# One-hots of two heads turned together, 128 columns wide, with the work of the first batch placed anew

## The chip, the cores and the metric

The kernel runs on one core of a Trainium2 chip. A core has five engines that run side by side and wait for each other through semaphores: TensorE (PE, matmuls; weight loads are listed as PEld), VectorE (DVE), ScalarE (ACT), GpSimd (POOL) and SyncE (SP), which here only issues DMAs. Each engine works through its own instructions in the order in which the program gave them. Matmuls write to PSUM, which only VectorE and ScalarE of the other engines read here. The metric is the device time of one execution in microseconds (us); the kernel before took 343.95 us (median of three runs, 343.53 to 344.48).

## What is computed

Four batches of eight attention heads with 768 queries and keys of 64 elements, followed by a gated feed-forward network (FFN). Every query and every key is assigned to the nearest of 16 centroids of its head, and a query only attends to keys with the same centroid:

```python
q_assign = np.argmax(np.einsum('bhsd,hcd->bhsc', q_n, c_n), axis=-1)
k_assign = np.argmax(np.einsum('bhsd,hcd->bhsc', k_n, c_n), axis=-1)
mask = q_assign[:, :, :, None] == k_assign[:, :, None, :]
scores = np.where(mask, scale * np.matmul(q, k.transpose(0, 1, 3, 2)), -1000000000.0)
attn = softmax(scores);  x = np.matmul(attn, v)        # then rows of 512 = 8 heads x 64
out = (sigmoid(x @ w_gate) * (x @ w_val)) @ w_out      # 3072 x 512 -> 1536 -> 512
```

## The kernel before

**Pairs and heads.** Two heads make a pair; a batch has four pairs (p = 0 to 3, e = 0 or 1 in the pair). For each head a tile `T` holds, in columns, six 128-blocks of keys and six of queries. Its rows 0 to 63 hold the high half of each element in 16 bits and rows 64 to 127 the low half; from these the logits against the centroids are made. Then rows 64 to 79 are overwritten by the one-hot of the assignment: 1 for the chosen centroid of a key, and for a query -1920 (`MASK`) for every centroid but its own. A score matmul then contracts over 80 rows, so that the mask is added to the product of key and query.

**Scores.** A head has 12 steps, each one score matmul `sc` (L512: one 128-block of keys against 384 queries), an exponential `es` on ScalarE (L517), and three matmuls `av` (L529) which use `es` as weights against the values. `av` follows its score by `LA` steps (`la0` for batch 0, `la1` for the others, both 2). The last pair of each batch is done in two halves of the queries, six steps each. In all 384 steps; batch 0 has steps 0 to 95. Head 4 starts at step 48, head 5 at 60, head 6 at 72, head 7 at 78.

**FFN.** `ffn_run` mixes matmuls of the FFN into the steps: each step gets a credit (`ns0` to `ns3` by batch, in ns), and pieces of a queue are issued until it is used up. The queue first gets work at step 92. What is left after the last step runs as the tail.

**Preparation of a head.** Batch 0 and the first pair of batch 1 are prepared with TensorE by `pieces` (L577): `hi` casts the high half (L588), `lo` subtracts it to get the low half (L595), `tu` turns it with six TensorE transposes into PSUM (L606), `ev` copies that to `T` (L615 ScalarE, L617 VectorE), `lg` makes logits (L299), `pk` picks the one-hot (L629, L631), `ot` turns the one-hot (L643), and `pl` copies it to rows 64 to 79 of `T`, once for keys (L653, VectorE) and once for queries, scaled by `MASK` (L655 ScalarE, L657 VectorE). In the one-hot tile a pair has 128 columns: four slots of 32, two for each head, with 16 used. `ot` turns the 64 columns of one head at a time, into partitions 0 to 63 or 64 to 127 (32 columns for the halved first head). The other pairs are prepared by `pair_prep` (L766), which turns by DMA transposes on SP and brings the one-hots to their rows by small DMAs (`hop`, L355).

**The order of the work.** The program is written out by hand. `plan(name, ...)` and `at(step, ...)` put each piece behind a step; the numbers in the dictionary `SCHED` say which step (h0 to h7 are batch 0's heads, g0 and g1 batch 1's first two; `vs`, `vc` the value sums and casts, `w`, `wo` the weights' loads on GpSimd's queue). Names that end in E choose an engine: A ScalarE, D VectorE, P GpSimd; otherwise `hi` and `ev` are on VectorE and `lo` on GpSimd. Before step 0, `dummies` (L570) issues matmuls on zeros: `dm0` of 512 columns, `dm1` to `dm4` of 128. PSUM is split into a ring of four banks, which scores, FFN and logits share, two buffers for `av`, and two for turns and FFN outputs.

Of the kernel before, what the change touches and what calls it, by code (L numbers as in the profile page):

```python
# [8 lines left out]
FP = mybir.dt.float32  # L9
HP = mybir.dt.float16  # L10
AF = mybir.ActivationFunctionType
ALU = mybir.AluOpType
# [4 lines left out]
    "halved0": 1, "npe": 1, "npe0": 4, "vs00": 5, "h1tu0": 0, "h1ev0": 0, "h1tu1": 0,  # L17
    "h1ev1": 1, "h1lg": 2, "h1pk": 3, "h1ot": 6, "h1pl0": 10, "h1pl1": 11, "h2hi0": 0,
    "h2lo0": 0, "h2hi1": 0, "h2lo1": 1, "h2tu0": 2, "h2ev0": 3, "h2tu1": 3, "h2ev1": 10,
    "h2lg": 10, "h2pk": 12, "h2ot": 13, "h2pl0": 15, "h2pl1": 20, "h3hi0": 0, "h3lo0": 4,  # L20
    "h3hi1": 1, "h3lo1": 4, "h3tu0": 11, "h3ev0": 12, "h3tu1": 15, "h3ev1": 16, "h3lg": 18,
    "h3pk": 19, "h3ot": 20, "h3pl0": 24, "h3pl1": 30, "vc01": 13, "vs01": 24, "h4hi0": 4,
    "h4lo0": 15, "h4hi1": 15, "h4lo1": 20, "h4tu0": 27, "h4ev0": 28, "h4tu1": 30, "h4ev1": 31,
    "h4lg": 31, "h4pk": 36, "h4ot": 40, "h4pl0": 44, "h4pl1": 41, "h5hi0": 21, "h5lo0": 30,
    "h5hi1": 29, "h5lo1": 33, "h5tu0": 38, "h5ev0": 38, "h5tu1": 41, "h5ev1": 41, "h5lg": 43,
    "h5pk": 44, "h5ot": 49, "h5pl0": 49, "h5pl1": 58, "vc02": 26, "vs02": 37, "h6hi0": 26,
    "h6lo0": 40, "h6hi1": 42, "h6lo1": 44, "h6tu0": 51, "h6ev0": 55, "h6tu1": 54, "h6ev1": 59,
    "h6lg": 63, "h6pk": 65, "h6ot": 67, "h6pl0": 69, "h6pl1": 69, "h7hi0": 22, "h7lo0": 40,
    "h7hi1": 45, "h7lo1": 53, "h7tu0": 60, "h7ev0": 62, "h7tu1": 58, "h7ev1": 64, "h7lg": 65,
    "h7pk": 65, "h7ot": 69, "h7pl0": 75, "h7pl1": 72, "vc03": 47, "vs03": 69, "g0hi0": 57,  # L30
    "g0lo0": 66, "g0hi1": 67, "g0lo1": 70, "g0tu0": 77, "g0ev0": 78, "g0tu1": 81, "g0ev1": 81,
    "g0lg": 81, "g0pk": 81, "g0ot": 87, "g0pl0": 87, "g0pl1": 92, "g1hi0": 69, "g1lo0": 78,
    "g1hi1": 77, "g1lo1": 78, "g1tu0": 85, "g1ev0": 86, "g1tu1": 87, "g1ev1": 90, "g1lg": 93,
    "g1pk": 93, "g1ot": 100, "g1pl0": 100, "g1pl1": 106, "w00": 3, "w01": 13, "w10": 26,
    "w11": 20, "w20": 15, "w21": 35, "w30": 39, "w31": 65, "wo0": 73, "wo1": 91, "b1p0vc": -18,
    "b1p0vs": -11, "b1p0vu": -2, "b1p0vt": 5, "b1p0ld": -80, "b1p1sp00": -59, "b1p1sp01": -53,
    "b1p1tn0": -50, "b1p1lg0": -35, "b1p1pk0": -31, "b1p1sp10": -48, "b1p1sp11": -43,
    "b1p1tn1": -40, "b1p1lg1": -24, "b1p1pk1": -24, "b1p1ot": -22, "b1p1hp0": -21,
    "b1p1hp1": -6, "b1p1vc": -19, "b1p1vs": -20, "b1p1vu": -14, "b1p1vt": -1, "b1p1ld": -78,
    "b1p2sp00": -58, "b1p2sp01": -54, "b1p2tn0": -54, "b1p2lg0": -32, "b1p2pk0": -29,  # L40
    "b1p2sp10": -54, "b1p2sp11": -47, "b1p2tn1": -43, "b1p2lg1": -28, "b1p2pk1": -26,
    "b1p2ot": -26, "b1p2hp0": -9, "b1p2hp1": -23, "b1p2vc": -18, "b1p2vs": -12, "b1p2vu": -8,
    "b1p2vt": 3, "b1p2ld": -86, "b1p3sp00": -57, "b1p3sp01": -55, "b1p3tn0": -49,
    "b1p3lg0": -39, "b1p3pk0": -30, "b1p3sp10": -56, "b1p3sp11": -44, "b1p3tn1": -40,
    "b1p3lg1": -31, "b1p3pk1": -27, "b1p3ot": -25, "b1p3hp0": -21, "b1p3hp1": -14,
    "b1p3vc": -15, "b1p3vs": -14, "b1p3vu": -5, "b1p3vt": 4, "b1p3ld": -79, "b2sp00": -59,
    "b2sp01": -50, "b2tn0": -48, "b2lg0": -37, "b2pk0": -36, "b2sp10": -52, "b2sp11": -44,
    "b2tn1": -40, "b2lg1": -27, "b2pk1": -27, "b2ot": -19, "b2hp0": -11, "b2hp1": -17,
    "b2vc": -17, "b2vs": -15, "b2vu": -13, "b2vt": 4, "b2ld": -83, "xt30": 2, "xt31": 5,
    "lag00": 8, "lag01": 7, "lag10": 6, "lag11": 10, "ns0": 530, "ns1": 470, "ns2": 500,  # L50
    "ns3": 440, "dm0": 12, "dm1": 2, "dm2": 6, "dm3": 11, "dm4": 2, "la0": 2, "la1": 2,
    "lgop": 0, "h2pl1E": "A", "h2lo0E": "D", "h4hi0E": "P", "h1ev0E": "A", "h3hi0E": "A",
    "h4pl1E": "A", "g0hi1E": "A", "h5lo1E": "D", "h5ev0E": "A", "h6hi0E": "A", "g0ev1E": "A",
    "h7hi1E": "P", "h4hi1E": "P", "h4lo0E": "D", "g1hi0E": "A", "h7hi0E": "A", "h3pl1E": "A",
    "h4lo1E": "D", "h5lo0E": "D", "g1lo0E": "D", "h5hi1E": "A", "h3ev0E": "A", "h3hi1E": "A",
    "h5hi0E": "P", "g0hi0E": "P",
# [4 lines left out]
def kernel(  # L61
# [68 lines left out]
    ohs = [const.tile([128, NCH, 128], HP, name=f"oh{i}") for i in range(3)]  # L130

    def oh_zero(i):
        POOL.memset(ohs[i].rearrange("p c (s x) -> p (c s) x", x=32)[:, :, NCL:32], 0.0)

    oh_zero(1)
    POOL.memset(ones, 1.0)

    def raw(side):
        return rawp.tile([128, 2, NCH, 64], FP, tag=f"{side}raw", name=f"{side}raw")

    SRC = {"q": q, "k": k, "v": v}

# [739 lines left out]
```

## Time and profile before

| | |
|---|---|
| median of three runs | 343.95 us (343.53 to 344.48) |
| the profiled execution | 342.54 us, its span 340.8 us |
| TensorE busy | 330.0 us, 3382 matmuls |
| ScalarE busy | 236.3 us |
| VectorE busy | 181.5 us |
| GpSimd busy | 107.8 us |
| first score, score 96, last score start at | 10.6, 68.1, 287.7 us |
| narrow one-hot turns (L643) | 66 matmuls: 54 of 64 columns, 12 of 32 |

A row of the timeline gives start, duration, engine, line, operation, the tile written and those read, and how many instructions were merged into the row. A matmul's duration includes its way through the array, so the pace of TensorE is read from the starts of two matmuls in sequence. A row of the waits says who waited for whom, how long in all, how often, and the longest. A row by stretch has the stretch, its length, and the busy time of each engine with the number of instructions.

### The profile page before, as it was taken

The page shows a single profiled execution, that of the slowest core. Times are in us where ns is not written, and L with a number is a line of the kernel's source. Part 1 is how long each engine was busy: PE and PEld are TensorE (multiplying, and loading weights), DVE is VectorE, ACT ScalarE, POOL GpSimd, SP SyncE. Part 2 cuts the span into 40 slices and gives each one's busy share as a digit, 9 for nine tenths or more (in the row PEclk, how much of TensorE's full clock was granted, in tenths as well). Part 3 has the DMA queues.
Part 4 walks back from the last instruction along what each step waited for, and adds up shares of the span by engine and source line. Part 5 has one row for each costly group of instructions (what it writes and reads, how often), then busy time and mean ns, then how long its engine had stood idle before and what let it go on. Part 6 is the DMA issues. An engine that isn't in the chain of part 4 may idle for free.

```text
span 340.8 us, 8867 instructions
## 1 busy us (share of the span) xinstructions
PE 330.0 (97%) x3382; PEld 206.7 (61%) x3382; DVE 181.5 (53%) x482; ACT 236.3 (69%) x542; POOL 107.8 (32%) x162
## 2 busy tenths in 40 slices
PE   8888998999999999999999999999999999999996
PEld 4665675666656665566656665666556665554654
DVE  3775569976736566456635656456544342341431
ACT  4789988777767887788768776788768876331321
POOL 4655658534133243423433232424301011000000
PEclk9999999999999999999999999999999999999999
DMA  7969978996587628777767448762643012101002
GB/s 224 376 148 174 244 188 130 205 213 167 95 200 204 145 78 119 187 174 195 94 171 189 87 160 126 211 125 52 98 119 79 11 24 69 49 2 62 33 0 92
DMA packets 79610, 45.33 MB, mean 133 GB/s; under 512 B 57616, under 2 KB 76624, under 8 KB 79568
## 3 DMA queue, kind: packets, MB, share of 16 engines
q1 hardware_dynamic: 73632, 40.02, 48.6%
q0 software_dynamic: 5792, 4.72, 9.6%
q8 instruction: 26, 0.43, 0.5%
q14 instruction: 16, 0.13, 0.1%
q10 hardware_dynamic: 144, 0.03, 0.0%
HBM read 28.34 MB, written 6.29 MB: 102 GB/s over the span
## 4 chain that ended last, share of the span: by engine, by line
PE 89%; DVE 5%; ACT 3%; issue 1%; DMA 1%; POOL 0%; DVEq 0%; ACTq 0%; POOLq 0%
PE v L385 19%; PE g L370 18%; PE o L402 17%; PE sc L512 16%; PE av L529 10%; PE lg L308 2%; PE wm L575 2%; ACT es L517 2%; PE t_ps L606 1%; DVE hl L595 1%; PE oh_ps L643 1%; DMA xTb<-xp 1%; PE o_end L426 1%; PE lg L299 1%; DVE T L617 1%
## 5 line engine op out<-in xcount | busy, mean ns | idle before, releaser
L517 ACT ACTIVATE es<-sc 128x384 f16<-128x384 f32 x384 | 172.7, 492 | 46.3 <-PE sc L512 24.6
L512 PE MATMUL sc<-T 80*128 80x384 f16 x384 | 117.1, 327 | 0.5 <-DVE T L657 0.2
L529 PEld LDWEIGHTS <-es 128*128 128x128 f16 x1152 | 79.7, 98 | 52.5 <-ACT es L517 11.8
L529 PE MATMUL av<-va,es 128*128 128x65 f16 x1152 | 98.1, 194 | 2.4 <-ACT es L517 1.5
L390 DVE SCALAR_TENSOR_TENSOR hT<-th,v 128x384 f16<-128x384 f32 x96 | 53.1, 553 | 70.7 <-PE av L529 43.9
L370 PE MATMUL g<-xTb,wg 128*128 128x384 f16 x384 | 78.2, 325 | 0.5 <-DVE sv L244 0.2
L385 PE MATMUL v<-xTb,wv 128*128 128x384 f16 x384 | 78.1, 325 | 0.2
L272 POOL TENSOR_TENSOR xp<-t,rec 128x384 f16<-128x384 f32 (+1 forms) x40 | 28.6, 716 | 130.8 <-DVE rec L269 81.3
L402 PE MATMUL o<-wo,hT 128*128 128x512 f16 x276 | 68.6, 378 | 0.0
L376 ACT ACTIVATE th<-g 128x384 f32<-128x384 f32 x96 | 47.1, 491 | 26.0 <-DVE hT L390 18.0
L370 PEld LDWEIGHTS <-wg 128*128 128x128 f16 x384 | 37.3, 97 | 22.1 <-issue 1.0
L385 PEld LDWEIGHTS <-wv 128*128 128x128 f16 x384 | 37.3, 97 | 21.3 <-issue 0.8
L402 PEld LDWEIGHTS <-hT 128*128 128x128 f16 x276 | 26.7, 97 | 23.3
L512 PEld LDWEIGHTS <-T 80*128 80x128 f16 x384 | 37.0, 96 | 1.2 <-DVE T L657 0.4
L267 DVE TENSOR_TENSOR t<-av,sv 128x390 f32<-128x390 f32 (+1 forms) x40 | 19.2, 479 | 29.2 <-PE av L529 26.8
L774 POOL TENSOR_TENSOR hl<-qraw,hl 128x384 f16<-128x384 f32 x22 | 20.6, 937 | 32.9 <-DVE hl L773 32.8
L774 POOL TENSOR_TENSOR hl<-kraw,hl 128x384 f16<-128x384 f32 x22 | 20.1, 919 | 12.3 <-issue 8.9
L411 ACT ACTIVATE ob<-o 128x512 f32<-128x512 f32 x15 | 9.0, 597 | 14.6 <-PE o L402 14.6
L322 DVE TENSOR_TENSOR lgs<-lg,lglo 128x192 f32<-128x192 f32 x22 | 7.8, 355 | 19.7 <-ACT lglo L314 19.2
L221 POOL CAST va<-vraw 128x768 f16<-128x768 f32 x16 | 14.2, 888 | 0.0
L409 DVE TENSOR_SCALAR ob<-o 128x512 f32<-128x512 f32 x8 | 5.5, 689 | 11.9 <-PE o L402 11.9
L606 PE MATMUL t_ps<-identh,hl 128*128 128x128 f16 x120 | 10.2, 221 | 0.4 <-DVE T L653 0.4
(79 smaller groups left out, 232.7 us busy)
## 6 DMA issues: line engine op xcount, KB each, us to landing
vraw<-in_v_dram SPq DMA_DIRECT2D x16, 384.0 KB, 6.1
out_dram<-ob SPq DMA_DIRECT2D x23, 256.0 KB, 2.7
kraw<-in_k_dram SPq DMA_DIRECT2D x15, 384.0 KB, 4.4
qraw<-in_q_dram SPq DMA_DIRECT2D x15, 384.0 KB, 5.6
wg<-in_moe_w_gate_dram POOLq DMA_DIRECT2D x4, 384.0 KB, 7.8
wv<-in_moe_w_val_dram POOLq DMA_DIRECT2D x4, 384.0 KB, 6.2
wo<-in_moe_w_out_dram POOLq DMA_DIRECT2D x2, 768.0 KB, 9.4
T<-ohT SPq DMA_DIRECT2D x44, 24.0 KB, 1.9
```

Of the source, the lines that this page charges most:

```text
L221: (cast or POOL.tensor_copy)(va[:, :, :, 0:64], RAW["v", b, p])
L267: DVE.tensor_tensor(t[:, 0:nq, :], av, sv, ALU.add)
L272: (eng or POOL).tensor_tensor(x, t[:, 0:nq, 0:64], bcast(rec[:, 0:nq], 64), ALU.mult)
L370: PE.matmul(out=g[:, 0:n], lhsT=wg[fc // WQ][:, dc, fc % WQ, :], rhs=xT[:, dc, t0 : t0 + n], start=(dc == 0), stop=(dc == NDC - 1),)
L376: ACT.activation(th[:, 0:n], g[:, 0:n], AF.Tanh, scale=0.5)
L385: PE.matmul(out=w[:, 0:n], lhsT=wv[fc // WQ][:, dc, fc % WQ, :], rhs=xT[:, dc, t0 : t0 + n], start=(dc == 0), stop=(dc == NDC - 1),)
L390: DVE.scalar_tensor_tensor(hT[:, fc, 0:n], st[0][:, 0:n], 1.0, w[:, 0:n], ALU.add, ALU.mult)
L402: PE.matmul(out=o, lhsT=hT[:, fc, bass.ts(t, 128)], rhs=wo[fc // 6][:, fc % 6, :], start=(fc == 0), stop=(fc == NFC - 1),)
L512: PE.matmul(out=sc.rearrange("p (c t) -> p c t", t=128), lhsT=s["k"], rhs=s["q"], start=True, stop=True,)
L517: ACT.activation(es, sc, AF.Exp, scale=SCALE)
L529: PE.matmul(out=av[:, s["c0"] + i, :], lhsT=s["es"][:, bass.ts(i, 128)], rhs=VA[b, p][:, e, s["j"], :], start=(first and i == 0), stop=(la ...
L774: POOL.tensor_tensor(hl[:, :, 64:128], r, hl[:, :, 0:64], ALU.subtract)
```

## The change

In batch 0, pairs 2 and 3 (heads 4 to 7) turn the one-hots of both heads at once (`ott`), after the second head's pick. One copy (`oe`) takes all 128 partitions from PSUM to a tile `ohT`, and multiplies the query slots by `MASK` through a column of scales (`slot_f`). Four DMAs for each pair (`hp`, 24 KB each, SP's queue) bring the slots to rows 64 to 79 of the `T` tiles. The other heads keep `ot` and `pl`, but turn all 128 columns of the pair's one-hot tile, and `pl` reads its own 16 rows; the one-hot tiles are therefore cleared as a whole at the start.

`do_scores` can issue 128-column matmuls on zeros ahead of a score, into the score's bank; thirteen steps get 27 in all (`nd`). `la0` and `la1` go from 2 to 3. The dummies before step 0 go from 12 wide and 21 narrow (`dm4` among them) to 7 wide and 15 narrow. Nearly all places of preparation are set anew, several pieces change their engine, and the credits of the FFN for each step change.

```diff
-    "vs00": 5, "h3ot": 20, "h4lo0": 15, "h4lo1": 20, "h4tu0": 27, "h4lg": 31, "h4pk": 36,
-    "h4ot": 40, "h4pl0": 44, "h4pl1": 41, "h5pk": 44, "h5ot": 49, "h5pl0": 49, "h5pl1": 58,
-    "h6tu0": 51, "h6ev0": 55, "h6lg": 63, "h6pk": 65, "h6ot": 67, "h7ev0": 62, "h7pk": 65,
-    "h7ot": 69, "h7pl0": 75, "h7pl1": 72, "b1p1ld": -78, "b1p1sp00": -59,
-    "ns0": 530, "ns1": 470, "ns2": 500, "ns3": 440, "dm0": 12, "dm1": 2, "dm2": 6, "dm3": 11,
-    "la0": 2, "la1": 2,
-    "h2pl1E": "A", "h2lo0E": "D", "h4pl1E": "A", "h5lo1E": "D", "h5ev0E": "A", "h6hi0E": "A",
-    "h4lo0E": "D", "h7hi0E": "A", "h4lo1E": "D", "g1lo0E": "D", "h5hi1E": "A", "h3ev0E": "A",
+    "om02": 2, "om03": 2, "vs00": 0, "h3ot": 23, "h4lo0": 9, "h4lo1": 10, "h4tu0": 12,
+    "h4lg": 18, "h4pk": 23, "h4hp": 43, "h5pk": 33, "h5ot": 34, "h5oe": 34, "h5hp": 36,
+    "h6tu0": 39, "h6ev0": 39, "h6lg": 45, "h6pk": 46, "h6hp": 63, "h7ev0": 44, "h7pk": 52,
+    "h7ot": 55, "h7oe": 62, "h7hp": 68, "b1p1ld": -74, "b1p1sp00": -62,
+    "ns0": 515, "ns1": 470, "ns2": 480, "ns3": 410, "dm0": 7, "dm1": 1, "dm2": 2, "dm3": 10,
+    "la0": 3, "la1": 3,
+    "h2hi1E": "A", "h4hi1E": "A", "h4ev1E": "A", "h6hi0E": "P", "h6lo0E": "D", "h7lo0E": "D",
+    "g0lo0E": "D", "g0lo1E": "D", "nd70": 2, "nd48": 3, "nd37": 3, "nd40": 3, "nd67": 2,
+    "nd51": 1, "nd80": 2, "nd52": 1, "nd25": 2, "nd5": 1, "nd9": 2, "nd34": 2, "nd30": 3,
...
+    slot_f = const.tile([128, 1], FP, name="slot_f")
+
     def oh_zero(i):
-        POOL.memset(ohs[i].rearrange("p c (s x) -> p (c s) x", x=32)[:, :, NCL:32], 0.0)
+        POOL.memset(ohs[i], 0.0)
...
+    for i in range(4):
+        POOL.memset(slot_f[32 * i : 32 * i + 32], MASK if i % 2 else 1.0)
...
     def do_scores(s):
         sc = bank(384, name="sc")
+        for _ in range(SCHED.get(f"nd{step_no[0]}", 0)):
+            PE.matmul(
+                out=sc[:, 0:128], lhsT=warm[:, 0:128], rhs=warm[:, 0:128], start=True, stop=True
+            )
...
         def ot(part=0):
             n = NCH // parts
-            st["oh", part] = []
-            for r0_, m in ((64 * e, 64),) if parts == 1 else ((0, 32), (32, 32)):
-                ps = turns(128 * n, name="oh_ps")
-                st["oh", part].append(ps)
-                for c in range(n):
-                    PE.transpose(
-                        ps[r0_ : r0_ + m, bass.ts(c, 128)],
-                        ohx[b, p][:, n * part + c, r0_ : r0_ + m], identh,
-                    )
+            ps = st["oh", part] = turns(128 * n, name="oh_ps")
+            for c in range(n):
+                PE.transpose(ps[:, bass.ts(c, 128)], ohx[b, p][:, n * part + c, :], identh)
...
+        def ott():
+            ps = st["oh"] = turns(name="oh_ps")
+            for c in range(NCH):
+                PE.transpose(ps[:, bass.ts(c, 128)], ohx[b, p][:, c, :], identh)
+
+        def oe(eng=None):
+            r0_, r1_ = (0, 128) if mode[b, p] == 2 else (64 * e, 64 * e + 64)
+            if mode[b, p] == 2 or e == 0:
+                oht[b, p] = ohp.tile([128, NCH, 128], HP, tag="ohT", name="ohT")
+            dst = oht[b, p][r0_:r1_].rearrange("p c t -> p (c t)")
+            if eng is ACT:
+                ACT.activation(dst, st["oh"][r0_:r1_], AF.Copy, scale=slot_f[r0_:r1_])
+            else:
+                DVE.tensor_scalar(dst, st["oh"][r0_:r1_], slot_f[r0_:r1_], None, ALU.mult)
+
+        def hp():
+            for s in range(2):
+                hop(oht[b, p], 2 * e + s, T[b, h], 6 * s, 6)
+
+        if b + p and mode[b, p]:
+            d = dict(hi=hi, lo=lo, tu=tu, ev=ev, lg=lg, pk=pk, hp=hp)
+            if mode[b, p] == 1 or e:
+                d.update(ot=ott, oe=oe)
+            return d
```

## The prediction, made before the changed kernel was run

> **What bounds the kernel now.** I read the page first: TensorE is busy nearly throughout, but that row is no measure of its pace.
>
> ```profile
> span 340.8 us, 8867 instructions
> ...
> PE   8888998999999999999999999999999999999996
> ```
>
> So I asked for the five engines by stretch. Columns: length, then busy time of PE, weight loads, VectorE, ScalarE, GpSimd.
>
> ```profile
> 10.30:18.00 7.70, 6.39 (x103) 5.04 (x100) 5.78 (x17) 4.88 (x11) 5.29 (x7) 1.00 1.06 382
> 18.00:46.50 28.50, 26.02 (x403) 17.82 (x400) 17.11 (x41) 26.43 (x61) 16.20 (x24) 1.00 1.00 175
> 46.50:61.50 15.00, 13.33 (x226) 9.31 (x224) 13.88 (x32) 12.34 (x30) 10.86 (x14) 1.00 0.82 167
> ...
> 75.00:290.00 215.00, 214.53 (x2137) 133.34 (x2136) 112.86 (x314) 162.89 (x380) 62.50 (x85) 1.00 0.57 128
> ```
>
> From 75 us on TensorE streams: in the timeline a 384-column matmul is followed by the next 0.16 us later, with hardly a gap. Before that there is no FFN to fill it. ScalarE is busy 26.4 of 28.5 us between 18 and 46.5 us, VectorE 13.9 of 15.0 us between 46.5 and 61.5 us. TensorE waits there, as its waits say (total us, times, longest):
>
> ```profile
> PEld L529 <- ACT es L517: 11.4, 40, 0.7
> ```
>
> The chain of work that ended last shows who holds the time (start, length, what). From 10.3 to 66.5 us its pieces sum to TensorE 30, VectorE 14, ScalarE 8 and unexplained issue 2 us.
>
> ```profile
> 31.59 0.81 ACT T L655
> 37.74 0.81 ACT T L655
> 51.64 0.55 DVE T L653
> 52.22 0.56 DVE T L657
> 57.00 2.86 DVE hl L595
> ```
>
> The first four are evacuations of one-hots, the last a subtraction that took 2.94 us where the same form elsewhere took 0.55. Three more places of the timeline carry my numbers: the start, and a narrow turn between two other matmuls.
>
> ```profile
> 1.32 5.52 PE L575 MATMUL wm<-warm 128*128 128x512 f16 x14 [1.32 <-POOL warm L124]
> 4.54 0.96 DVE L595 TENSOR_TENSOR hl<-kraw,hl 128x192 f16<-128x192 f32 x2
> 6.62 0.53 PE L606 MATMUL t_ps<-identh,hl 128*128 128x128 f16 x3
> ```
>
> ```profile
> 16.78 0.25 PE L529 MATMUL av<-va,es 128*128 128x65 f16 x3
> 16.97 0.52 PE L643 MATMUL oh_ps<-identh,oh 128*64 128x128 f16 x6
> 17.42 0.34 PE L512 MATMUL sc<-T 80*128 80x384 f16 x1
> ```
>
> **The change, step by step**, against the profiled execution: 342.54 us, span 340.8.
>
> *Start.* Twelve wide dummies at 0.43 us each keep TensorE until 6.62 us, while the first half of the key residue is done at 5.02 (4.54 plus half of 0.96). Seven end at 1.32 + 7 x 0.43 = 4.3 us, so the first turn starts near 5.1 us: 1.5 us earlier. The last turns of the group then wait for GpSimd's two residues (4.72 to 5.90) and run at half rate. Past the first scores GpSimd is late next: head 2's key residue moves onto it (0.93 for VectorE's 0.56), head 3's keys stand before the turn of step 3, and each clearing of a whole one-hot buffer grows from 0.42 us to some 0.74 (the 512-element memset took 0.52, a 128-element one 0.20), plus four 0.10 us memsets of the scale column. The first two clearings lie in GpSimd's idle 1.95 and 2.01 us and cost nothing; the third counts. The bounds are -1.5 (all kept) and +0.5 (half rate lasts through the first scores); I take **-1.0**, nearer to the row of the dummies.
>
> *Turns.* Between the last value matmul and the narrow turn lie 0.19 us for three matmuls that elsewhere take 0.09; six narrow turns take 0.45 where six 128-wide ones (14.83 to 15.16) take 0.33. So one narrow group costs 0.10 + 0.12 = 0.22 us more; nine groups 2.0 us. Two groups vanish, 2 x 0.33 = 0.67. Two of the nine lie at 62 and 72.5 us, where little else waits: -0.4. The rest, 2.2 us, lie where ScalarE or VectorE holds the end and count here by what those leave: bounds 0 and -2.2, I take **-0.6, and -0.4 for the late two**. The Trainium skill, page "TensorE: Matmul & The Clock Gate", section "LDWEIGHTS (loading the stationary operand)", says that a weight load lasts as long as its columns, about columns/1.2 ns. By it, wider turns would cost 53 ns more each, some 2.2 us over 42 turns. The trace has 109 ns for 64 columns and 97 for 128, so the rows decide against it.
>
> *ScalarE, 18 to 46.5 us.* Beside the scores' exponentials (start to start 0.38: seven from 32.42 end at 35.21) it now has eight other instructions: three one-hot evacuations that hold it 0.82 each, two turn copies at 0.68, three casts at 0.40, 5.0 us. By the new places two are left (head 4's query copy, head 3's one-hot), 1.5 us. So 3.5 us go; VectorE takes some of it and has 11 us idle there. TensorE can save no more than it now loses there, about 7.9 us of gaps beyond its streaming pace. A third score in flight instead of a second (the lookahead rises by one) turns short ScalarE delays into no TensorE wait, while four PSUM ring banks stay four. Bounds -0.5 and -5.0; as TensorE and ScalarE alternate on the chain, I take 60% of 3.5: **-2.1**.
>
> *VectorE, 46.5 to 61.5 us.* Its 13.9 us: heads 6 and 7 are prepared there. By the new places their copies and picks come before, one evacuation of both heads (0.56) replaces four (2.2), and the 2.94 us subtraction of batch 1's head 1 goes to GpSimd; two others (batch 1's head 0) come in, 0.55 each. The instructions that the new order puts on steps 65 to 86, each by the mean of its form now, sum to 7.4 us. VectorE then no longer holds the end; ScalarE (12.3 us busy, less by pitch) does. TensorE's gaps there, 4.6 us, bound it: 0 and -4.6. I take **-2.6**.
>
> *Dummies before scores.* 27 matmuls of 128 columns, 56 ns each as the turns show: 1.5 us. They stand on steps 5 to 80, where the next score would mostly wait for ScalarE anyway; if TensorE held the end, all would count. By TensorE's share of the chain (30 of 55 us) it would be 0.8; most of them stand in ScalarE's stretch, so less: **+0.6**, bounds 0 and +1.5.
>
> *Hops.* Eight DMAs of 24 KB on SP, which landed in 1.9 us (median) elsewhere, behind an output transpose and before loads of batch 1. They wait for the evacuation at step 34 or 62 alone, and the heads are used at steps 48 and 72. At over half a us per step there are over 5 us. I take **0**, bounds 0 and +3.5 (four issues at 0.4 plus a landing) for each pair. Behind them stand the loads of batch 1's second pair, first read at step 58, some 10 us after the hops issue; they land in 4.4 to 6.1 us.
>
> *Later places, FFN shares per step (500 to 480, 440 to 410 ns).* The streaming is moved from steps to the tail; both are TensorE at full pace. **0**, bounds -1.0 and +1.0 from the 3 us of gaps after 100 us.
>
> Sum: -1.0 - 0.6 - 0.4 - 2.1 - 2.6 + 0.6 = -6.1, so 336.4 for a profiled execution. The profiled one lay 1.4 us under the median of the three runs; the prediction for the median is 343.95 - 6.1 = **337.8 us**.
>
> **The rivals.**
> 1. *Half the gain.* As VectorE sheds its part, GpSimd or ScalarE holds the same stretch; the terms of the two stretches halve, 4.7 to 2.3: 340.2, up to 342.9. For it speaks that the stretches are coupled; against, that ScalarE sheds work too.
> 2. *Late full rate.* Turns at 6.62 us follow at 0.11 us, those after 7.16 at 0.06: the clock came 5.8 us after the first matmul of unbroken dummies. With a pause after 4.3 us it may come as much later as the row allows: 5.8 us after 5.1, so 10.9 instead of 7.16. In 3.7 us at half rate TensorE loses at most the half of what it streams, 1.9 us: 339.7. The same page, section "Part 1: The HAM clock gate", says that the rate follows activity in free-running windows of 3.4 us; by it the switch would come one window later, at 10.6 us, near the same 339.7. No run here shows yet which.
> 3. *Nothing kept:* what ScalarE and VectorE give up lies beside TensorE's own pace and the dummies eat the turns: 343 to 345.
> 4. *Slower: stretched subtractions.* Place: five key or query residues on VectorE (heads 5, 6, 7, batch 1's head 0 twice) beside GpSimd. The row at 56.91 us shows 2.94 us while GpSimd ran four instructions back to back; others show 0.55 and 0.71. Price 2.4 us each. With two the time is 342.6, with three 345.0: from three on the chain it decides, and four give 347. Against: one of six was stretched so now. The Trainium skill, "SBUF — State Buffer", section "SBUF: two separate sides", says VectorE and GpSimd take a shared port pair as an exclusive lock, which agrees with this row.
> 5. *Slower: hops late.* If SP is held, head 4's and 6's first scores wait, at the bound 3.5 us each: 344.8, beyond it slower. Against: more than 5 us of lead.
>
> **How the numbers follow.** Forecast 0.50 (its own range 333 to 341), rival 1 0.15, 2 0.10, 3 0.07, 4 0.11, 5 0.07. About 0.3% (1 us) can be told from no change by these runs. Faster: the first three, 0.75; same 0.07; slower 0.11 + 0.07 = 0.18. The range reaches from the forecast's bounds (both stretches kept to 80%, and the start whole: near 332.5) to the edge of no change, 345.0, and leaves out the slower cases and little below.
>
> **What would show it.** Turns of six at 0.33 us, with 0.09 before; the first real turn near 5.1 us and first score near 9.5; score matmul 96 (from 0) starting near 62 us instead of 68.1; the stretches' ScalarE and VectorE share falling while TensorE's gaps shrink; no wait of TensorE on a hop. I am wrong if score 96 comes no earlier, if the gaps after 75 us grow, or if subtractions on VectorE last over 2 us.

## The result: 1.6% slower

The changed kernel took 349.63 us in the median (348.05 to 350.06, four runs) beside 344.0 us of the kernel before (343.53 to 344.48): a ratio of 1.0155, with an interval of 1.0121 to 1.019. Slower, by 5.6 us and clear of the noise, where 337.8 was forecast; the range ended at 345.0. Medians and ranges here and below are of all runs of a kernel, while a ratio leaves out runs that were over 1.5% above that kernel's fastest.

The profiled execution took 348.05 us. From its page, the lines that answer those of before:

```profile
span 346.3 us, 8803 instructions
...
PEclk9999998998999999999999999999999999999999
...
PE 77%; DMA 12%; DVE 3%; POOL 2%; SPq 2%; issue 2%; ACT 1%; POOLq 0%; DVEq 0%
```

Two things are new. In the shares of the chain TensorE had 89% and DMA 1%; now DMA has 12%. And the row of the granted clock, all nines before, has two eights. The waits of TensorE on transfers (total, times, longest) say which transfers:

```profile
PE sc L520 <- DMA T<-ohT: 6.3, 5, 1.7
PE lg L312 <- DMA T<-hl: 3.1, 1, 3.1
PE g L374 <- DMA xTb<-xp: 0.4, 1, 0.4
```

The kernel before has no wait of TensorE on a DMA there. `T<-ohT` is the hop of a one-hot to its rows, `T<-hl` the DMA transpose of a head's halves, `xTb<-xp` the transpose of the output that the FFN reads.

The stretches, cut at the same scores as those of before (length, then PE, weight loads, VectorE, ScalarE, GpSimd, clock):

```profile
16.50:43.00 26.50, 24.42 (x454) 20.01 (x451) 18.17 (x49) 22.34 (x53) 17.17 (x26) 1.00 1.05 196
43.00:57.70 14.70, 12.52 (x171) 8.18 (x170) 7.47 (x19) 11.88 (x31) 8.05 (x11) 0.88 0.97 180
...
71.30:285.00 213.70, 206.38 (x2068) 128.97 (x2067) 111.21 (x312) 158.80 (x372) 62.15 (x84) 0.99 0.62 129
```

ScalarE's share of the first fell from 26.4 of 28.5 us to 22.3 of 26.5, VectorE's of the second from 13.9 of 15.0 to 7.5 of 14.7: batch 0 was relieved as meant. But the second has a clock of 0.88, and in the last, the streaming one, TensorE now stands for 7 us where it stood for half a microsecond.

By the starts of the scores: the first comes at 9.11 us (10.59 before), score 96 at 64.34 (68.11). Batch 0 gained 3.8 us. From score 96 to the last matmul it is 278.9 us (269.6 before), so 9.3 are lost behind it. The pitch of TensorE's starts shows where (a stop is the time between two starts, less the usual pitch of the first of them): it stops 3.23 us at 78 us (`T<-hl` of batch 1's third pair), 1.71 at 107.5, 0.54 and 0.81 at 145, 1.83 at 220.5, 8.1 us together; a stretch at half clock near 82 us adds 1.7. In batch 0 it stops too, 0.85 us ahead of head 4 and 1.88 ahead of head 6.

SyncE's own queue around the stop ahead of head 6 shows why that hop was late. First SP's issues, then the piece of the chain that ends in the stop:

```profile
43.69 0.57 SPq L154 DMA_DIRECT2D kraw<-in_k_dram  x1
44.31 1.32 SPq L154 DMA_DIRECT2D qraw<-in_q_dram  x1
45.67 0.47 SPq L154 DMA_DIRECT2D vraw<-in_v_dram  x1
46.40 2.42 SPq L360 DMA_DIRECT2D T<-ohT  x4
```

```profile
47.02 4.04 DMA T<-ohT
```

The hops of heads 6 and 7 (24 KB each) are issued behind three loads of 384 KB. The second of head 6's two, issued at 47.02 us, lands at 51.06, 4.04 us on the chain where 1.9 was the median before. They land in the order of issue: the last of the three loads at 50.45 us, the four hops from 50.83 to 51.72. The page "DMA: Bandwidth & Descriptors" of the Trainium skill, section "Queues, rings and completion order", says that each DMA engine consumes the descriptors of one such queue in the order of its ring; a hop whose last packets stand behind 1.2 MB is what that would look like, and the order of issue is what the experiments change.

After the stop, TensorE goes on at half its clock. Four windows of 3.41 us, two with a stop and each one's successor:

```profile
47.86:51.27 3.41, 1.34 (x21) 0.93 (x19) 1.77 (x4) 1.76 (x5) 2.56 (x3) 1.00 0.96 272
51.27:54.68 3.41, 3.41 (x29) 2.23 (x29) 1.46 (x4) 2.94 (x7) 1.66 (x3) 0.50 0.66 105
78.58:81.99 3.41, 0.58 (x17) 0.52 (x18) 0.12 (x1) 0.27 (x2) 0.82 (x1) 1.00 1.34 103
81.99:85.40 3.41, 3.41 (x19) 1.73 (x17) 1.88 (x6) 1.51 (x4) 0.00 (x0) 0.50 0.63 126
```

TensorE is busy 1.34 and 0.58 us of the windows with a stop, and each next one has a clock of 0.50: up to 1.7 us more for each.

### The profile page after: what moved, and what is told of

Same layout as the page of the kernel before. It is cut to its first block, busy times and chain, and to the rows that moved or that the text cites. A ratio compares the mean times of both kernels' runs of the same rounds, so it can differ in the third digit from the quotient of the medians.

```text
span 346.3 us, 8803 instructions
## 1 busy us (share of the span) xinstructions
PE 327.7 (95%) x3380; PEld 208.2 (60%) x3380; DVE 176.1 (51%) x479; ACT 233.3 (67%) x537; POOL 110.3 (32%) x168
## 4 chain that ended last, share of the span: by engine, by line
PE 77%; DMA 12%; DVE 3%; POOL 2%; SPq 2%; issue 2%; ACT 1%; POOLq 0%; DVEq 0%
PE v L389 17%; PE g L374 16%; PE sc L520 15%; PE o L406 14%; PE av L537 9%; DMA T<-ohT 6%; DMA T<-hl 5%; PE lg L312 2%; POOL hl L603 2%; PE lg L303 1%; DMA cen<-in_centroids_dram 1%; PE t_ps L614 1%; PE o_end L430 1%; SPq L559 1%; SPq L360 1%
## 5 line engine op out<-in xcount | busy, mean ns | idle before, releaser
L520 PE MATMUL sc<-T 80*128 80x384 f16 x384 | 118.3, 331 | 7.0 <-DMA T<-ohT 6.3
L537 PEld LDWEIGHTS <-es 128*128 128x128 f16 x1152 | 82.3, 99 | 47.4 <-issue 2.7
L406 PE MATMUL o<-wo,hT 128*128 128x512 f16 x276 | 67.8, 378 | 0.0
L380 ACT ACTIVATE th<-g 128x384 f32<-128x384 f32 x96 | 47.1, 491 | 26.1 <-DVE hT L394 17.8
L225 POOL CAST va<-vraw 128x768 f16<-128x768 f32 x16 | 13.7, 858 | 0.0
L312 PE MATMUL lg<-cm,T 128*128 128x32 f16 x264 | 10.0, 176 | 3.1 <-DMA T<-hl 3.1
```

The lines of the kernel that those rows point to most:

```text
L312: PE.matmul(out=lg[:, bass.ts(c, 32)], lhsT=t[:, c, :], rhs=cm[:, h].rearrange("p s n -> p (s n)"), start=True, stop=True,)
L380: ACT.activation(th[:, 0:n], g[:, 0:n], AF.Tanh, scale=0.5)
L406: PE.matmul(out=o, lhsT=hT[:, fc, bass.ts(t, 128)], rhs=wo[fc // 6][:, fc % 6, :], start=(fc == 0), stop=(fc == NFC - 1),)
L520: PE.matmul(out=sc.rearrange("p (c t) -> p c t", t=128), lhsT=s["k"], rhs=s["q"], start=True, stop=True,)
L537: PE.matmul(out=av[:, s["c0"] + i, :], lhsT=s["es"][:, bass.ts(i, 128)], rhs=VA[b, p][:, e, s["j"], :], start=(first and i == 0), stop=(la ...
```

## The experiments

The theory: *queue order*. SP issues one list of transfers. A short one that stands behind three input loads lands some us late; the change moved the hops behind the loads (heads 6 and 7 at steps 63 and 68, batch 1's loads at 58; in the later batches 8 steps ahead of their use instead of 11, where the loads stand 11 ahead) and, with the lookahead of three, the output transpose too (step 182, loads at 181). Each stop costs its own length and perhaps a window at half clock. Against it stand: the wide turns or the dummies cost TensorE more than thought; the loads of the output weights (`wo`, 768 KB each, on GpSimd's queue) at steps 83 and 91, 73 and 91 before, take the bandwidth; or the whole of the later places is worse, whatever the order.

### First group: the hops, the weights' loads, the turns

**a_hops**, the changed kernel with the hops of heads 6 and 7 ahead of the loads at step 58:

```diff
-    "h6hp": 63, "h7oe": 62, "h7hp": 68,
+    "h6hp": 57, "h7oe": 56, "h7hp": 57,
```

> The changed kernel with the copy of heads 6 and 7 at step 56 instead of 62 and their four hops at step 57 instead of 63 and 68, so that SP issues them ahead of batch 1's third pair of loads (step 58). Theory H (the hops wait behind 1.2 MB of loads in the DMA queue): TensorE's wait on a hop near 47 us (1.9 us) goes, and with it the stretch at half clock after it (51.5 to 54.9 us, about 1.6 us): 346 to 346.5 us against 349.6. Rival (the hop is late because its copy is late on VectorE, or lands slowly wherever it stands): the wait stays within 0.5 us of 1.9 and the time within 1 us of 349.6.

Measured: 344.93 us (341.87 to 348.39, ten runs), ratio 1.0041 (1.0002 to 1.008). Of the 5.6 us lost, about 4 came back. In the profile, of the fastest of the ten runs (span 340.1 us), the stop ahead of head 6 is gone, its hops land in 1.8 to 2.8 us, score 96 starts at 61.27 us, 6.8 earlier than in the kernel before, and nothing runs at half clock; later stops remain, of 0.95 us at step 111, 2.36 ahead of score 144, 0.38 and 0.82 around score 192 and 1.72 ahead of score 288. The edit moves the copy and the hops earlier as well as ahead of the loads, so for head 6 it doesn't part the two.

**a_wo**, the changed kernel with the two loads of `wo` earlier, and **a_both**, both edits:

```diff
-    "wo0": 83, "wo1": 91,
+    "wo0": 73, "wo1": 83,
```

> The changed kernel with the two output weight loads at steps 73 and 83 instead of 83 and 91. Theory W (batch 1's DMA transposes near 63 us land after 17.8 us because both weight loads are in flight): the wait of the logits on the transpose (3.1 us near 78 us) shrinks below 1 us, and the half clock after it (82.2 to 85.6 us) goes: 345 to 346 us. Rival (the transposes are late from their own places on SP, or from the loads of inputs): the wait stays above 2.5 us and the time within 1 us of 349.6.

> Both edits at once. If the two waits are separate, the gains add: 342 to 343.5 us, level with the kernel before. If they are one shortage of DMA time, curing one moves the wait to the other, and this run is no better than the better of the two alone.

Measured: 349.5 us (346.93 to 354.62), ratio 1.0164 (1.01 to 1.0229), and 350.96 us (348.77 to 353.3), ratio 1.0233 (1.0174 to 1.0292). The waits of a_wo:

```profile
PE g L374 <- DMA xTb<-xp: 5.3, 2, 4.8
PE lg L312 <- DMA T<-hl: 0.5, 1, 0.5
```

The 3.1 us on `T<-hl` shrink to 0.5, so the loads of `wo` do bear on it; but the output transpose at 60.5 us, which they now stand beside, is 4.8 us late. The lateness moved to another short transfer, and nothing was won. That stands against `wo` as a cause to be repaired by moving it alone, not against its having a part. In a_both, too, the output transpose is late, by 6.2 us; the gains do not add, and it is 6 us slower than a_hops. That is the case which its expectation called one shortage of DMA time, so around these loads that rival stands.

**b_wide**, the kernel before with only the wide turns and the clearing of the whole tiles:

```diff
-        POOL.memset(ohs[i].rearrange("p c (s x) -> p (c s) x", x=32)[:, :, NCL:32], 0.0)
+        POOL.memset(ohs[i], 0.0)
...
-                for c in range(n):
-                    PE.transpose(
-                        ps[r0_ : r0_ + m, bass.ts(c, 128)],
-                        ohx[b, p][:, n * part + c, r0_ : r0_ + m], identh,
-                    )
...
+            for c in range(n):
+                PE.transpose(ps[:, bass.ts(c, 128)], ohx[b, p][:, n * part + c, :], identh)
...
```

> The kernel before with all one-hot turns 128 columns wide and the one-hot tiles cleared as a whole, nothing else. Theory T (a narrow group costs TensorE 0.22 us more, nine groups 2.0 us, of which about half is on the path): 342.4 to 343.5 us against 344.0, groups of six at 0.33 us with 0.09 before. Rival (wider weight loads cost more, 53 ns each): 345 to 346 us.

Measured: 342.87 us beside 342.9 (ten runs), ratio 0.9988 (0.9963 to 1.0013). Alone, the turns change nothing that can be measured: they neither carry the loss nor, alone, a gain of 1 us beyond doubt.

### Second group: the later batches

**a_hp**, a_hops with the eight places of hops and their one-hots in the later batches as before; **b_hp**, the reverse, the kernel before with the eight places of the changed one:

```diff
# a_hp, beside the edit of a_hops
-    "b1p2ot": -25, "b1p2hp0": -7, "b1p2hp1": -14,
-    "b2lg1": -24, "b2pk1": -24, "b2ot": -16, "b2hp0": -8, "b2hp1": -14,
+    "b1p2ot": -26, "b1p2hp0": -9, "b1p2hp1": -23,
+    "b2lg1": -27, "b2pk1": -27, "b2ot": -19, "b2hp0": -11, "b2hp1": -17,
...
# b_hp, on the kernel before
-    "b1p2ot": -26, "b1p2hp0": -9, "b1p2hp1": -23,
-    "b2lg1": -27, "b2pk1": -27, "b2ot": -19, "b2hp0": -11, "b2hp1": -17,
+    "b1p2ot": -25, "b1p2hp0": -7, "b1p2hp1": -14,
+    "b2lg1": -24, "b2pk1": -24, "b2ot": -16, "b2hp0": -8, "b2hp1": -14,
```

> The changed kernel with heads 6 and 7's hops early (as in the run of the early hops, 344.9 us) and, besides, eight places of batch 1's third pair and of the first pairs of batches 2 and 3 as in the kernel before: their last hops 2 or 3 steps earlier, and the picks and turns ahead of them. Theory H (a hop issued close to its head, behind loads, holds TensorE): the waits at the heads that start at steps 144, 192 and 288 (2.4, 0.8 and 1.7 us in that run) fall below 0.5 us each: 340 to 341.5 us. Rival (these heads wait because DMA is short of time whatever the place): the waits stay, 344 to 346 us.

> The kernel before with only the eight places of the changed kernel (last hops of batch 1's third pair at 7 instead of 9 steps before use, of batches 2 and 3 at 8 instead of 11, with their picks and turns). Theory H: waits of 1 to 2.4 us each at the heads of steps 144, 192 and 288 appear where the kernel before has none: 345.5 to 348 us against 343. Rival (the places only hurt where batch 0 is faster): within 1 us of the kernel before.

Measured: a_hp 352.76 us (350.0 to 354.17), ratio 1.0264 (1.0211 to 1.0318), where 340 to 341.5 or 344 to 346 was expected. b_hp 356.55 us (356.03 to 358.99), ratio 1.0375 (1.0321 to 1.0428), and not 345.5 to 348. The second is the clearest: eight numbers of the schedule, no other work, and the kernel before loses 12 us. SP's issues around the loads at step 181, in the kernel before:

```profile
136.98 1.19 SPq L551 DMA_TRANSPOSE xTb<-xp  x1
138.22 1.21 SPq L356 DMA_DIRECT2D T<-ohT  x2
139.47 0.58 SPq L150 DMA_DIRECT2D kraw<-in_k_dram  x1
```

and in b_hp, with its wait of TensorE:

```profile
139.41 1.20 SPq L551 DMA_TRANSPOSE xTb<-xp  x1
140.66 0.58 SPq L150 DMA_DIRECT2D kraw<-in_k_dram  x1
...
142.81 1.16 SPq L356 DMA_DIRECT2D T<-ohT  x2
```

```profile
PE sc L512 <- DMA T<-ohT: 9.7, 3, 4.9
```

The hop has moved behind the loads, and score 192 stands for 5.03 us. a_hp shows the other half: the waits on hops fall from 4.8 to 1.2 us, but with the lookahead of three the output transpose is issued behind the loads and now comes directly after them; the FFN waits on it for 3.6 us at step 191 and 3.3 at 288, each followed by half clock (6.8 and 3.4 us).

**a_hl**, a_hops with all places and credits from batch 1 on as before, lookahead and dummies as changed; **a_bare**, a_hl with lookahead two and no dummies ahead of scores:

```diff
# a_hl, beside the edit of a_hops
-    "b1p0ld": -73, "b1p1ld": -74, "b1p3ld": -77, "ns0": 515, "ns2": 480, "ns3": 410,
+    "b1p0ld": -80, "b1p1ld": -78, "b1p3ld": -79, "ns0": 530, "ns2": 500, "ns3": 440,
...
# a_bare, beside that of a_hl
-    "la0": 3, "la1": 3, "nd70": 2, "nd48": 3,
+    "la0": 2, "la1": 2,
...
```

> As the run before, but with all places of batches 1 to 3, the output weights' loads and the FFN credits as in the kernel before; of the change are left the batch 0 part, the turns, the dummies and the lookahead. Theory H: as good as the run with the eight places, 339.5 to 342 us, since nothing else in the late places costs. Rival (the late places were needed to go with a batch 0 that ends 4 us earlier): waits on transposes or on the FFN's input appear, 343 to 347 us.

> The run with all late places of the kernel before, also without the 27 dummies and with a lookahead of 2. Theory L (the third score in flight and the dummies give 0.5 to 2 us): 0.5 to 2 us slower than that run, with more waits of TensorE on exponentials before 60 us. Rival (dummies cost what they last, 1.5 us, and lookahead gives nothing, since four ring banks are the limit): 1 to 1.5 us faster.

Measured: a_hl 365.26 us (362.62 to 372.39), ratio 1.0588 (1.0525 to 1.0652); a_bare 349.48 us (348.88 to 355.6), ratio 1.0149 (1.0101 to 1.0197). Neither is in a range that was expected: 339.5 to 342 or 343 to 347 for a_hl, and for a_bare at most 2 us from it. The old places do not repair the changed kernel. In a_hl they make it worse: batch 1's loads then stand ahead of head 4's hop (step 42; head 4 starts 3.94 us late), and with the lookahead of three the output transposes stand behind the loads at 181 and 277 (stops of 3.9 and 5.6 us). With a lookahead of two (a_bare) the first of these stops is gone and the second 1.2 us; a_bare is 16 us faster, though its profile, of the slowest of its runs, also stands 1.8 us ahead of head 4 and 2.9 us for a GpSimd subtraction. `T<-hl` at step 85 is 6.7 us late in both: that transpose stands behind three loads and took 11.6 and 12.5 us while loads of weights were in flight; these two do not tell which of the two holds it.

### Third group: moving the loads instead

**a_ld**, a_hops with the loads of batches 2 and 3 five steps later:

```diff
-    "b2ld": -83,
+    "b2ld": -78,
```

> The changed kernel with heads 6 and 7's hops early, and the loads of batches 2 and 3 five steps later (78 instead of 83 steps before use), so that on SP the output transposes and hops of the heads that start at steps 144, 192 and 288 stand ahead of the three loads of 384 KB and not behind. Theory Q (what stands behind such loads in the queue lands some 4 us later): the waits there (2.4, 1.2 and 1.7 us in the run of the early hops, 344.9 us) fall below 0.5 us each, no new wait on the output transposes: 339.5 to 341.5 us. Rival (DMA is short of time, the order does not matter, or the loads now come late): 344 to 347 us, waits elsewhere.

Measured: **334.87 us** (334.47 to 335.15), ratio 0.9748 (0.9705 to 0.979): 8.9 us faster than the kernel before measured beside it (343.78). Its page, and SP's issues at the same place:

```profile
span 332.7 us, 8801 instructions
...
PEclk9999999999999999999999999999999999999999
...
PE 91%; DVE 2%; POOL 2%; ACT 2%; issue 1%; DMA 1%; SPq 0%; POOLq 0%; DVEq 0%
```

```profile
130.10 1.20 SPq L559 DMA_TRANSPOSE xTb<-xp  x1
...
131.99 1.15 SPq L360 DMA_DIRECT2D T<-ohT  x2
133.18 0.58 SPq L154 DMA_DIRECT2D kraw<-in_k_dram  x1
```

Transpose, hop, then the loads: no wait of TensorE on a DMA is over 0.3 us, and nothing runs at half clock. The account closes: the changed kernel's span is 13.6 us longer (346.3 - 332.7); its waits on DMA are 9.8 us (6.3 + 3.1 + 0.4) and its two windows at half clock 2 x 1.7, 13.2 together. It says how much the stops cost, not that one cause made them all: the wait of 3.1 us on `T<-hl` is taken up again below.

**b_la3**, the kernel before with only the lookahead of three:

```diff
-    "la0": 2, "la1": 2,
+    "la0": 3, "la1": 3,
```

> The kernel before with the lookahead at 3 for all batches, nothing else. By theory Q the output transposes of the fourth pair's first half now stand behind the loads of steps 181 and 277: two waits of the FFN on them of 3 us or more, half clock after each: 348 to 352 us, and score 96 between 66 and 68.1 us. Rival (a lookahead of 3 only takes waits away): 341.5 to 343.5 us.

Measured: 357.92 us (355.61 to 358.88), ratio 1.041 (1.0352 to 1.0467).

```profile
PE g L370 <- DMA xTb<-xp: 9.7, 2, 5.2
```

Hop, loads, transpose: the FFN waits for 4.66 us at step 191 and 5.36 at 284. The hop ahead of score 144 is 1.0 us late too. What the lookahead alone is worth in batch 0 this profile does not show: scores 8 to 48 take 22.30 us (22.67 before), but two windows at half clock follow, from 40.1 to 46.9 us, and score 96 starts at 68.72 us (68.11).

**a_la2**, a_ld with the later lookahead at two and head 4's hop eight steps earlier; **a_nond**, a_ld without the 27 dummies ahead of scores:

```diff
# a_la2, on a_ld
-    "h4hp": 43, "la1": 3,
+    "h4hp": 35, "la1": 2,
...
# a_nond, on a_ld
-    "nd70": 2, "nd48": 3, "nd37": 3, "nd40": 3, "nd67": 2, "nd51": 1, "nd80": 2, "nd52": 1,
-    "nd25": 2, "nd5": 1, "nd9": 2, "nd34": 2, "nd30": 3,
```

> As the run with the later loads, with a lookahead of 2 in batches 1 to 3 and head 4's two hops ahead of head 5's. Theory Q: the output transposes come one step earlier and head 4 does not wait (0.6 to 0.9 us near 38 us): 0.5 to 1.5 us faster than that run. Rival (lookahead of 3 hides waits in batches 1 to 3): 0.5 to 2 us slower.

> As the run with the later loads, without the 27 dummy matmuls before scores. If they cost what they last on a TensorE that is the limit: 1.5 us faster. If they lie in waits for ScalarE: within 0.5 us. If they keep the clock up through the waits of batch 0: slower by 1.5 us or more, with half clock before 60 us.

Measured: a_la2 338.98 us (335.16 to 342.75, two runs near each end), ratio 0.9764 (0.9699 to 0.983), with 3.2 us on `T<-hl` at step 96 in its profile, of a run near the upper end, and two windows at half clock behind it (its two faster runs, 335.16 and 335.68 us, lie within 1 us of a_ld); a_nond 336.64 us (335.08 to 338.48), ratio 0.9801 (0.9734 to 0.9868). Without dummies the best version was 1.8 us slower, not faster; its profile has a stop of 1.08 us ahead of head 4 and then a window at half clock. The intervals of a_nond and a_ld overlap, so that dummies help is likely and not shown; that they cost 0.6 us is not what the runs say.

### Fourth group: how the loss divides

**a_ldo**, the changed kernel with `b2ld` at -78 and nothing else; **a_la1**, the changed kernel with `la1` back at 2 and nothing else; **a_ld4**, a_ld with `h4hp` 35 instead of 43; **b_ld**, the kernel before with `b2ld` at -78:

```diff
# a_ldo on the changed kernel, b_ld on the kernel before
-    "b2ld": -83,
+    "b2ld": -78,
...
# a_la1, on the changed kernel
-    "la1": 3,
+    "la1": 2,
...
# a_ld4, on a_ld
-    "h4hp": 43,
+    "h4hp": 35,
```

> The changed kernel with one number changed: the loads of the third and fourth batch five steps later (-83 to -78), hops of heads 6 and 7 left where the change put them (on the queue behind the loads of batch 1's third pair). Queue order in the later batches carries the loss: then the stops after 100 us go, those at heads 4 and 6 and batch 1's third pair stay (0.9 + 1.9 + 3.2 us with two half-rate windows of 3.4 us, 1.7 us each), so 334.9 + 6.0 + 3.4 = 344.3, range 341 to 347, no wait of the gate matmuls on xTb. The hops of heads 6 and 7 carry all of it: 349 to 350, as the changed kernel.

> The changed kernel with the later batches' lookahead back at two, nothing else. The output transpose then stands ahead of the loads on SP's queue, the last hop of a pair still behind them. If the lookahead is what costs late: no wait of the gate matmuls on xTb, but the hop waits stay or grow: 345 to 352. If only the places of the hops cost: the same 349 to 350 as the changed kernel with the wait on xTb still there. If the lookahead costs nothing and only batch 0's hops do: 349 to 350.

> The best version so far (hops of heads 6 and 7 earlier, loads of batches 2 and 3 five steps later) with head 4's hop also earlier, step 43 to 35, lookahead left at three. Queue order: head 4's hop has no wait left in the best version (under 0.3 us), so 334.9 within 1 us. If the earlier hop delays the loads of batch 1's second pair or an output transpose: 336 to 342 with a wait of TensorE on T<-hl or xTb near 60 us.

> The kernel before with one number changed: the loads of the third and fourth batch five steps later (-83 to -78). It has no wait of TensorE on a DMA, and its short transfers stand ahead of these loads already, so later loads can gain nothing: 343 to 345. If the later loads are by themselves what made the best version fast, it gains too: 336 to 341, and the change's own part of the gain is that much smaller. If later loads come too late for the batch that reads them: slower, with a wait on T<-hl.

Measured: a_ldo 343.95 us in the median of ten runs, which fall into two groups, four of 337.4 to 339.8 and six of 343.8 to 346.9; the ratio of 0.9868 (0.9837 to 0.9899) is that of the lower group. What parts the groups is not known: runs of 339.4 and of 344.1 us have the same mean granted clock of 0.99. Its profiled execution (upper group) has

```profile
PE lg L312 <- DMA T<-hl: 3.8, 1, 3.8
PE sc L520 <- DMA T<-ohT: 2.9, 2, 2.6
```

and no stop behind step 111: one number repaired the later batches, as queue order says, and the stops ahead of heads 4 and 6 and at step 111 are left. a_la1: 353.81 us (352.7 to 355.61), ratio 1.0311 (1.0268 to 1.0355). The wait on `xTb` is gone, but the hop now comes directly behind the loads, and score 192 stands 5.30 us, score 288 3.68. The time lay above the 345 to 352 of the reading that has these waits: undoing the lookahead alone makes it worse by 4 us. a_ld4: 335.87 us (three runs of 334.7 to 336.9, one of 341.26), ratio 0.9772 (0.9728 to 0.9817), the same as a_ld. b_ld: 343.33 us, ratio 0.999 (0.9967 to 1.0013): later loads give the kernel before nothing. The gain of a_ld is the change's own.

### What they say together

Around the loads at step 181, in order of issue on SP, with TensorE's stop at step 191:

| kernel | order on SP | stop |
|---|---|---|
| before, b_ld, b_wide, a_bare | transpose, hop, loads | none |
| a_ld, a_ldo, a_ld4, a_la2, a_nond | transpose, hop, loads | none |
| changed | loads, transpose, hop | 0.54 + 0.81 us |
| a_hops | loads, transpose, hop | 0.38 + 0.82 us |
| a_wo, a_both | loads, transpose, hop | 0.67 + 0.82, 0.59 + 0.81 us |
| a_hp | hop, loads, transpose | 3.61 us, on the transpose |
| a_hl | hop, loads, transpose | 3.94 us, on the transpose |
| b_la3 | hop, loads, transpose | 4.66 us, on the transpose |
| b_hp | transpose, loads, hop | 5.03 us, on the hop |
| a_la1 | transpose, loads, hop | 5.30 us, on the hop |

What stands behind the loads is what TensorE waits for, in either kernel. Where both stand behind them it is only 1.3 us, and SP's issues in the changed kernel show two reasons:

```profile
139.01 0.58 SPq L154 DMA_DIRECT2D kraw<-in_k_dram  x1
...
140.66 1.20 SPq L559 DMA_TRANSPOSE xTb<-xp  x1
...
142.53 1.17 SPq L360 DMA_DIRECT2D T<-ohT  x2
```

With the transpose ahead of them the loads are issued only after it. In b_hp SP issues nothing from 137.9 us until the transpose at 139.41, and the first load comes 4.3 us before score 192 is due (its start less the stops); with the loads in front it comes 6.3 us before. And the loads land sooner, the last one 6.2 us after the first one's issue (8.2 in b_hp), and the first hop 7.4 us after it (9.1). Why they land sooner is not known.

The loss does not divide by simple sums. Against the kernel before measured beside each, the changed kernel is 5.6 us slower in the median, a_hops 2.0, a_ldo 0.5, and a_ld 8.9 faster: the hops of batch 0 alone give back 3.6 us, the later loads alone 5.2 (10 by the lower group of a_ldo), both 14.5. The profile of a_ldo has the stops ahead of head 6 and at step 111 longer than the changed kernel's (2.78 and 3.93 for 1.88 and 3.23 us), and both windows at half clock kept. Up to step 109 the order of these two programs is the same, so that much is the spread from one execution to another. That a stop costs a window more or not is part of the rest, which was not taken apart.

The largest stop of the changed kernel, 3.23 us on `T<-hl` at step 111, is not shown to be queue order. The awaited transpose is issued behind three loads in the kernel before and in a_ld as well, and there TensorE does not stop for it. What differs is how long it took: 6.1 us from issue to landing in the kernel before, 13.7 in a_ld, 17.8 in the changed kernel (63.52 to 81.36 us), where one load of `wo` was in flight until 70.70 us and the other, issued 0.8 us behind the transpose, until 81.92. In a_ld it landed within 0.7 us of the second load of `wo` too. That the two loads of weights hold it is likely, and a_wo, where its wait shrinks to 0.5 us, agrees; no run takes them out of this stretch, so the cause stays open. No edit was made at this stop in a_hops and a_ld: with batch 0's hops early it is 0.95 us in one and gone in the other.

## Why the prediction was wrong, step by step

**The forecast failed at two steps that were set at nothing: *Hops* and *Later places*.** In their place the runs showed stops of TensorE on short DMA transfers, 0.85 and 1.88 us in batch 0 and 8.1 us behind it, and two windows at half clock of 1.7 us each. The gains it summed were there.

*Start*, -1.0. The first score came 1.48 us earlier in the changed kernel, 2.10 in a_ld. But it varies from one execution to another: over the five profiles of the kernel before and its variants it starts at 9.8 to 10.6 us (10.0 in the mean), over the thirteen of the changed kernel and its variants at 8.5 to 9.1 (8.9). The first turns, and a later group of six with the score behind it:

```profile
5.04 0.50 PE L614 MATMUL t_ps<-identh,hl 128*128 128x128 f16 x3 [0.45 <-DVE hl L603]
...
15.81 0.50 PE L648 MATMUL oh_ps<-identh,oh 128*128 128x128 f16 x6
16.15 0.33 PE L520 MATMUL sc<-T 80*128 80x384 f16 x1
```

The first turn starts at 5.04 us (5.1 forecast), the first score at 9.11 (9.5). The step is right, and 1.2 us by the means is near what was taken.

*Turns*, -0.6 and -0.4. Six turns take 0.34 us from start to start (15.81 to 16.15), as forecast. Alone in b_wide they give -0.4 us, with an interval of -1.3 to +0.4: the working is right, its worth at most what was taken.

*ScalarE's stretch*, -2.1, and *VectorE's*, -2.6. With the queue in order (a_ld) scores 8 to 60 take 26.53 us for 28.29, so -1.8; scores 60 to 88 13.01 for 17.00, so -4.0. These stretches hold the turns and the dummies too, which the forecast priced apart. Both are right in place and sign. The second is under-sized: VectorE then has so little there that the bound of 4.6 was nearer than the 2.6 taken. In the changed kernel itself the stop ahead of head 6 and the window behind it ate most of it (15.48 us).

*Dummies*, +0.6. The sign is doubtful: without them a_ld was 1.8 us slower, with intervals that overlap.

*Hops*, 0. The working said that the hops wait for the evacuation alone and stand ahead of the loads. For heads 4 and 5 the order is so, and the landing of 1.9 us is not: their hops took 4.8 to 5.3 us with no load ahead of them on SP and two loads of weights in flight on GpSimd's queue, and head 4 is 0.85 us late. For heads 6 and 7 the order is false: their places, 63 and 68, are behind step 58, where batch 1's third pair is loaded, and the issues show it. From score 62 to the time when score 72 is due are 4.9 us, nearly the lead of five. But VectorE makes the copy only at 45.76 us, and the hops, issued from 46.40, have 2.9 us left. At 1.9 us they would have been in time; behind the loads they took 4.0 to 4.4. The bound of 3.5 us a pair was not passed in batch 0 (0.85 and 1.88), but the window at half clock behind the stop was in no term.

*Later places*, 0 with bounds of 1.0. This is the larger failure. The stretch behind score 96 was 9.3 us longer: 8.1 of stops and 1.7 of half clock. Of these, 4.9 us are the hops and the output transpose behind loads, which a_ldo takes away with one number; 3.2 and the half clock are the transpose at step 111, whose cause stays open. The working compared the amount of streaming, which indeed did not change (a_ld 269.05 us from score 96 to the last matmul, before 269.6), and did not follow SP's queue: hops placed 8 steps ahead of their use instead of 11 fall behind loads that stand 11 ahead, and a lookahead of three moves the output transpose by one step, past the loads at 181. The lookahead was priced for batch 0 only; in the later batches it alone costs 14 us in the kernel before (b_la3: 284.0 us from score 96 to the start of the last matmul, 269.4 before).

**The rivals.** *Hops late* (0.07) was the right mechanism at too few places: it was looked for at heads 4 and 6, and lay more in the later batches and on transposes. *Stretched subtractions* did not happen: VectorE's, at 21 to 48 us, took 0.53 to 1.03 us each in the changed kernel and a_ld, none over 2. *Half the gain* and *nothing kept* fall with a_ld: 8.9 us were there. *Late full rate* is half right. In the changed kernel the full rate is granted at 6.9 us, no later than before; in five of the thirteen profiles of it and its variants it came at 4.0 to 4.8 us and was taken away again for 3.4 us. In a_ldo the window from 4.30 to 7.71 us, with TensorE busy for 2.90 us of it, has the full rate, and the one to 11.12 us half of it. That is close to the 10.9 us which the rival gave as the end, but its price is small: score 4 starts at 14.72 us in a_ldo and at 14.37 in a_ld, which kept its rate.

**The range.** Its lower end, 332.5, does not follow from the terms that it names: with both stretches at 80% of their bounds and the start whole the sum is -9.6, which is 334.4 from the median and 333.0 from the profiled execution. Nothing hangs on it.

**What would show it.** Score 96 did come earlier (64.3, 62 forecast) and the gaps behind 75 us grew: one of the signs named for being wrong, and the one that decided.

## What to carry to other kernels

When pieces of a schedule are moved, write down each DMA queue in its new order and look at what each short, awaited transfer stands behind: here one number (loads five steps later) together with one pair's hops 6 and 11 steps earlier turned a loss of 5.6 us into a gain of 8.9. A lead in steps does not help a transfer that stands behind others in its queue; place the large prefetches, which have slack, behind the small transfers that a matmul waits for. And price a stop of TensorE with what may follow it: its own length, and up to 1.7 us for each window at half clock.

## What the runs showed of the hardware that was not expected

*Half clock after short stops.* The changes of the granted clock in a record lie multiples of 3.413 us apart. In the streaming stage (from 75 us on), over the eighteen profiles, each of the 13 such windows at full clock in which TensorE was busy for at most 1.55 us was followed by one at half clock, and none of the 19 with 1.73 to 2.5 us; one of the latter is in a_hops, where the edge of a window at 101.96 us cuts a stop of 2.36 us and leaves TensorE busy for 1.97 us. So where a stop falls among the windows decides its price. The Trainium skill, page "TensorE: Matmul & The Clock Gate", section "Part 1: The HAM clock gate", says that the windows are free-running and 3413 ns long, which these records agree with. After stops of 3.2 to 6.8 us half clock often lasted two windows or three (6.8, in a_hl and a_bare also 10.2 us). In batch 0, where matmuls are narrower, windows with 2.3 us busy were followed by half clock too: one in b_ld behind a stop of 0.75 us at step 81, which the kernel before has as well, without half clock in its own profile. Its 52 runs beside the experiments spread from 341.5 to 345.2 us, and the clock on record for each divides them: 27 with a mean granted clock of 0.999 or 1.0 took 342.65 us in the mean, 25 with 0.994 or 0.995 took 344.24. One window of 3.41 us at half clock lowers the mean by 0.005 and costs up to 1.7 us, so this is what such a window would do.

*A short transfer behind loads.* In b_hp and a_la1 a 24 KB hop directly behind three loads of 384 KB made TensorE stand 5.0 and 5.3 us, with the same hop ahead of them none. In all eighteen profiles the transfers issued behind these three loads landed after the last of them.

*Transposes beside loads of weights.* A DMA transpose `T<-hl` lands in 3.8 us in the median of the changed kernel. Behind three loads of 384 KB and with loads of weights in flight on GpSimd's queue it took 17.8 us there, 11.6 in a_hl and 12.5 in a_bare.
